# First chain rebuilt, second half's tiles normalised on GpSimd and turned behind the scores of slot 3, third unit's q products a slot later

## The chip, the cores and the metric

The kernel runs on one core of a Trainium2 chip, in one launch. The time is the device time in microseconds (us). Engines are called as the profile calls them: PE (TensorE, matrix products and turns), PEld (its weight loads), DVE (VectorE), ACT (ScalarE), POOL (GpSimd), SP (the queue that issues the transfers).

## What is computed

A transformer block with conditioned layer norms: attention over the last 512 entries of a cache, then a gated feed-forward net. S = 2048 rows of D = 512, 32 query heads on 8 key heads of 128.

```python
mod = (_silu(c) @ w_mod).reshape(c.shape[0], 6, 1, -1)
sa, ca, ga, sb, cb, gb = (mod[:, 0], mod[:, 1], mod[:, 2], mod[:, 3], mod[:, 4], mod[:, 5])
h = _layernorm(x, axis=-1) * (1 + ca) + sa
q = (h @ wq), by heads;  k, v = the last 512 rows of the caches
p = _softmax(q k^T * Dh ** -0.5);  x = x + ga * ((p v) @ wo)
h = _layernorm(x, axis=-1) * (1 + cb) + sb
x = x + gb * ((_gelu(h @ w_gate) * (h @ w_up)) @ w_down)
```

## The kernel before

Every product of two float32 matrices is made as three products of float16 halves: each operand is scaled, cut into a high half (a rounding) and a low half (what the rounding left), and `mm3` adds low by high, high by high and high by low in one PSUM bank. The scales come from norms that the kernel works out itself.

**Units and slots.** Attention is cut into units: one head times 512 rows (a quarter of the rows; the first two quarters are called first half and second half here, `qb` 0 and 1). A unit has four slots of 128 rows. The main loop runs over slots `t`: scores on PE (`ps`, two PSUM banks), the row maximum on DVE (`nm`), the exponential on ACT (`ee`), high half of `p` on ACT two slots later, low half on DVE three slots later, a transposing transfer (`pt`). Between these, `pop()` issues other products from a list: q products of coming units (`pq`), p times v (`po`), the output product (`py`). `EARLY` says how many are popped in each of the first eight slots. Everything else is put at a slot by `at(slot, fn)`: ("e", t) and ("d", t) on the way through slot t, a plain number behind its products, ("w", t) at its end. Within an engine instructions run in the order in which this code issues them.

**The first chain** is `begin()`, written out by hand; it runs from the first transfer to the first unit's q. Its steps: `silu` of the condition; the sum and factor columns `cols` of the layer norm, either by products on PE (`early_cols`, into `mps`) or by a multiply with a running sum on DVE (`mod_col`, L138); layer-norm statistics of four row tiles of the first half (`ln_stat`, `ln_power`) and the normalised tiles `xn`; their turn on PE (`turn`, into `pln`); norms of weights and k (`sumsq` on ACT, `sums` on PE); from these the scales `wsc`, `qsc`, `ksc` (`mod_scale`, `norm2`, `w_spread`); then for each of four column groups `dt` the scaled and shifted block, as float32 copy `hf` (`affine`, also written to DRAM), as high half (`direct`) and as low half (`low`); the weight's halves (`high_w`, `low_w`), k's halves, and `q_first`, in which `warm()` puts idle matmuls that keep PE going.

**The second half** needs the same for four further row tiles: `nb` holds their steps (statistics, root on GpSimd, normalisation into `xb`), `o1` the turn, copy and halves. The turn of the first column group has `fill(4)`, four idle matmuls, ahead of its third and fourth tile. The third unit (head 0, second half) is the first that needs them.

**Tables.** `PSE` names the slots whose exponential goes to a PSUM bank (tags "acc", "qa") and not to SBUF.

Of the kernel before, what the change touches and what calls it, by code (L numbers as in the profile page):

```python
# [18 lines left out]
P = 128  # L19
# [46 lines left out]
def block_kernel(ctx: ExitStack, tc: tile.TileContext, x, kT, v, wq, wo, wg, wu, wd, cT, wc, wm, out):  # L66
# [48 lines left out]
    half_ = const.tile([P, 1], F32, name="half_")  # L115
    nc.gpsimd.memset(half_, 0.5)
    ones = const.tile([P, 1], BF16, name="ones")
    nc.gpsimd.memset(ones, 1.0)
# [74 lines left out]

    def everywhere(out, m, n, fold=True):
        ps = bank("acc", "pst", NACC)
# [9 lines left out]

    def mod_scale(j, name, const_, m=None, mid=nop, between=nop):
        m, g, s = m or mod_max(j), little("mg", 2, 1), little("ms", 1, 1)
        everywhere(g, m, 2, False)
# [11 lines left out]

    def sums(m, n):
        ps = bank("acc", "pst", NACC)
        nc.tensor.matmul(ps[:, 0:n], ones.to_broadcast([P, P]), m[:, 0:n], start=True, stop=True)
        return ps
# [180 lines left out]
    def ln_first(i, act=False):  # L405
        st = {}

        def norm():
            if i < QT:
                xn[i] = tmp("xn")  # L410
                nc.vector.tensor_scalar(xn[i], acc[i], st["mv"][:, 0:1], st["rs"], op0=ALU.subtract, op1=ALU.mult)
            else:
                xn[i] = xn["b"][:, i - QT, :]
                nc.vector.tensor_scalar(xn[i], acc[i], st["mv"][:, 0:1], st["rs"], op0=ALU.subtract, op1=ALU.mult)

        def centre():
            if i < QT:
                xn[i] = tmp("xn")
            else:
                xn["b"] = pool.tile([P, QT, 512], F32, tag="pt", name="xb", bufs=NPT)  # L420
                xn[i] = xn["b"][:, 0, :]
            nc.scalar.activation(xn[i], acc[i], AF.Identity, bias=st["nm"], scale=1.0)

        def scale():
            nc.scalar.activation(xn[i], xn[i], AF.Copy, scale=st["rs"])

        pre = (lambda: ln_stat(acc[i], st, act), lambda: ln_power(st))
        return pre + ((centre, scale) if act else (norm,))

    def ln_out(qb, dt):  # L430
# [3 lines left out]

        def turn():
            st["ps"] = bank("acc", "pln", NACC)
            for i in range(QT):
                if qb and dt == 0 and i > 1:
                    fill(4)
                nc.tensor.transpose(st["ps"][:, i * P:(i + 1) * P], xn[qb * QT + i][:, dt * P:(dt + 1) * P], ident)  # L440
# [8 lines left out]

        def direct():  # L450
            nc.scalar.activation(block(0, name)[:, p, :], st["ps"], AF.Identity, scale=cols[:, 1, dt:dt + 1], bias=cols[:, 0, dt:dt + 1])

# [573 lines left out]
    def early_load(j, dt):  # L1026
        dma(wct[j][:, dt, :], wc[1, :, dt, :] if j else wm[0, dt])

# [23 lines left out]
    na = [ln_first(i, i >= 2) for i in range(QT)]  # L1052
    nb = [ln_first(QT + i, i == 0) for i in range(QT)]
    o0 = [ln_out(0, dt) for dt in range(KT)]
# [8 lines left out]
    def q_first(warm):  # L1063
        ps = bank("acc", "pq", NACC)
        for term, (a, b) in enumerate(((0, 0), (1, 0), (0, 2))):
            for kt in range(KT):
                w, m, p = SET[0][0], BK[0, ("b11", "b21")[kt // 2]], kt % 2
                nc.tensor.matmul(ps, w[:, a, kt * P:(kt + 1) * P], m[:, b + p, :], start=term + kt == 0, stop=term == 2 and kt == KT - 1)
            if term == 0:
                warm(3)  # L1070
        q_post(0, ps)

    def begin():
# [16 lines left out]
        def warm(n):  # L1090
            for _ in range(n):
                nc.tensor.matmul(wps, junk[:, 0:P], junk, start=True, stop=True)

        for dt in range(KT):
            mod_col(1, dt, wct[1][:, dt, :], sbc)
        for dt in range(KT):
            early_cols(mps, dt)
        m = {}
        pair_stat(0, m, 0)
        pair_stat(0, m, 1)  # L1100
        k0[1]()
        ts(cols[:, 1, :], cols[:, 1, :], 1.0, None, ALU.add)
        ts(cols[:, 0, :], mps[:, 0:KT], 1.0, None, ALU.mult)
        pst = {}

        def mid():
            o0[0][0]()
            pst["w"] = sums(m["m"], 2)
            o0[1][0]()
            pst["k"] = sums(k0[4]["m"], 1)  # L1110
            o0[2][0]()
            o0[3][0]()

        mod_scale(0, "ma", SCALE * TOP13 * TOP13, mod_max(0), mid)
        w = w_first(m["m"], pst["w"])
        o0[0][1](False)
        inv_k = k0[2](False, pst["k"])
        nc.vector.reciprocal(col("wsc", 0), w)
        inv_t, last = w_spread(0, m["m"], w)
        o0[0][3]()  # L1120
        high_w(0)
        for n in range(1, KT):
            o0[n][1](False)
            o0[n][3]()
            if n == 1:
                o0[0][2](nc.gpsimd)
            if n == 2:
                inv_k()
                inv_t()
                last()  # L1130
        warm(4)
        low_w(0)
        o0[1][2]()
        o0[2][2](nc.gpsimd)
        low_k = k0[3](True)
        o0[3][2]()
        low_k()
        nb[0][0]()
        nb[0][1]()
        high_w(1)  # L1140
        q_first(warm)
        v0[1]()
# [16 lines left out]
    at(("d", 4), lambda: o1[3][2]())  # L1159

# [400 lines left out]
    with tc.manual_schedule():  # L1561
        begin()
        nexty, invs = [], {}
        for t in range(T + TAIL):
# [278 lines left out]
```

## Time and profile before

| | us |
|---|---|
| median of 3 runs | 1729.52 (1729.38 to 1730.45) |
| profiled execution, device time | 1731.43 |
| its span, first to last instruction | 1729.6 |
| PE busy | 1709.0 (99% of the span) |
| DVE / ACT / POOL busy | 1426.7 / 1254.7 / 1090.0 |

Instants below are microseconds from the span's start. A profile row gives a group's start, its length, the engine, the line of the kernel, the operation, what it writes and reads, and in brackets how long the engine stood idle before it and what ended that.

### The profile page before, as it was taken

The numbers are of one execution on the slowest core, as the hardware profiler recorded it, in microseconds if no ns is written. First come the engines' busy times: TensorE is split into PE (matmuls) and PEld (weight loads), VectorE is DVE, ScalarE is ACT, GpSimd is POOL, SyncE is SP. The second block draws the span as 40 slices with busy tenths as digits, with TensorE's granted clock in tenths as the row PEclk, the third lists the DMA queues.
The fourth block names the chain that finished last, engine by engine and source line by source line (L and its number), as shares of the span: only waits on it lengthen the run. The fifth ranks groups of instructions, "written<-read, shape, count | busy, mean of one in ns | idle before, by whom it ended". The sixth has DMA issues, their size and how long they took to land.

```text
span 1729.6 us, 26339 instructions
## 1 busy us (share of the span) xinstructions
PE 1709.0 (99%) x8012; PEld 786.6 (45%) x8012; DVE 1426.7 (82%) x2476; ACT 1254.7 (73%) x2819; POOL 1090.0 (63%) x1328
## 2 busy tenths in 40 slices
PE   7999999999999999999999999999999999999999
PEld 5444444444444444444444444444444444444444
DVE  7888898888889899888788888888896788676666
ACT  6988788888888877888777877787785354455442
POOL 4879778777788984655665755757760345735424
PEclk9999999999999999999999999999999999999999
DMA  7999999999999998999999999999997556365353
GB/s 235 222 206 209 215 215 204 225 205 219 210 231 218 210 208 183 212 209 228 202 228 214 215 230 209 203 219 225 218 230 166 157 153 195 120 164 174 96 160 102
DMA packets 693454, 343.51 MB, mean 199 GB/s; under 512 B 579136, under 2 KB 602688, under 8 KB 693312
## 3 DMA queue, kind: packets, MB, share of 16 engines
q1 hardware_dynamic: 693024, 341.30, 85.7%
q8 instruction: 63, 1.03, 0.2%
q14 instruction: 79, 0.65, 0.1%
q10 hardware_dynamic: 288, 0.52, 0.1%
HBM read 137.50 MB, written 63.70 MB: 116 GB/s over the span
## 4 chain that ended last, share of the span: by engine, by line
PE 88%; DVE 4%; ACT 3%; DMA 2%; POOL 1%; issue 1%; SPq 0%; POOLq 0%; ACTq 0%; DVEq 0%
PE py L91 19%; PE po L91 17%; PE ps L91 17%; PE fa L91 8%; PE qa L91 8%; PE fc L91 4%; PE qc L91 4%; PE ya L91 3%; PE fb L91 2%; PE qb L91 2%; PE yc L91 2%; DMA pt<-p 1%; DVE p L1016 1%; ACT ee L999 1%; DVE nm L990 1%
## 5 line engine op out<-in xcount | busy, mean ns | idle before, releaser
L999 ACT ACTIVATE ee<-ps,nm 128x512 f32<-128x512 f32 x512 | 349.7, 683 | 185.6 <-DVE nm L990 180.3
L1016 DVE SCALAR_TENSOR_TENSOR p<-ee,rr,p 128x512 f16<-128x512 f32 x512 | 458.3, 895 | 8.1 <-ACT p L1011 7.6
L990 DVE TENSOR_REDUCE nm<-ps 128x1 f32<-128x512 f32 x512 | 350.3, 684 | 97.5 <-PE ps L91 95.2
L91 PE MATMUL ps<-k,qt 128*128 128x512 f16 x1536 | 414.9, 379 | 4.9 <-ACT ee L999 3.5
L1011 ACT ACTIVATE p<-ee,rr 128x512 f16<-128x512 f32 x512 | 364.0, 711 | 20.1 <-DVE rr L1007 11.3
L91 PE MATMUL po<-pt,v 128*128 128x512 f16 x1536 | 372.9, 379 | 2.6 <-DMA pt<-p 0.9
L91 PE MATMUL py<-wo,ot 128*128 128x512 f16 x1536 | 371.3, 379 | 0.0
L91 PEld LDWEIGHTS <-w 128*128 128x128 f16 x2184 | 213.5, 98 | 258.6 <-issue 0.9
L91 PEld LDWEIGHTS <-v 128*128 128x128 f16 x1536 | 150.0, 98 | 184.8 <-issue 2.8
L91 PEld LDWEIGHTS <-ot 128*128 128x128 f16 x1536 | 150.3, 98 | 181.3
L91 PEld LDWEIGHTS <-qt 128*128 128x128 f16 x1536 | 145.7, 98 | 176.4 <-issue 4.6
L1320 POOL TENSOR_TENSOR fg<-fg 128x512 f32<-128x512 f32 x48 | 62.9, 1310 | 134.6 <-DVE fg L1294 131.8
L748 DVE SCALAR_TENSOR_TENSOR ot<-po,ot 128x512 f16<-128x512 f32 x128 | 87.9, 687 | 39.2 <-ACT ot L747 38.7
L1304 ACT ACTIVATE at<-fg 128x512 f16<-128x512 f32 x92 | 56.3, 625 | 80.2 <-DVE fg L1294 60.7
L999 ACT ACTIVATION_READ_ACCUMULATOR ee<-ps,nm 128x1 f32 x512 | 100.1, 196 | 0.0
L960 DVE SCALAR_TENSOR_TENSOR acc<-py,ysc,acc 128x512 f32<-128x512 f32 x128 | 94.7, 740 | 5.3 <-PE py L91 5.3
L91 PE MATMUL qa<-t,w 128*128 128x512 f16 x348 | 84.9, 379 | 0.0
L236 POOL TENSOR_TENSOR lw<-lw,half__86 128x1 f32<-128x1 f32 x39 | 24.9, 639 | 94.7 <-DVE lw L186 94.6
L91 PE MATMUL fa<-t,w 128*128 128x512 f16 x336 | 81.6, 379 | 0.1
L747 ACT ACTIVATE ot<-po 128x512 f16<-128x512 f32 x128 | 73.9, 577 | 5.0 <-PE po L91 5.0
L403 POOL TENSOR_TENSOR rs<-rs,nhalf 128x1 f32<-128x1 f32 x32 | 18.7, 584 | 92.7 <-DVE rs L397 89.7
L91 PEld LDWEIGHTS <-wo 128*128 128x128 f16 x504 | 49.3, 98 | 59.6 <-issue 0.3
(243 smaller groups left out, 2813.8 us busy)
## 6 DMA issues: line engine op xcount, KB each, us to landing
w<-kept SPq DMA_DIRECT2D x123, 256.0 KB, 3.3
wo<-kept SPq DMA_DIRECT2D x72, 256.0 KB, 3.3
kept<-stage SPq DMA_DIRECT2D x67, 256.0 KB, 3.0
raw<-in_wo SPq DMA_DIRECT2D x56, 256.0 KB, 3.2
kept<-w SPq DMA_DIRECT2D x39, 256.0 KB, 3.4
rw<-in_wq SPq DMA_DIRECT2D x38, 256.0 KB, 3.1
hs<-hf SPq DMA_DIRECT2D x32, 256.0 KB, 2.7
pt<-p SPq DMA_TRANSPOSE x512, 3.5
```

The lines of the kernel that those rows point to most:

```text
L91: nc.tensor.matmul(ps, a, b, start=first and n == 0, stop=last and n == 2, skip_group_check=chain)
L236: nc.gpsimd.tensor_tensor(out, out, half_, op=ALU.pow)
L403: nc.gpsimd.tensor_tensor(st["rs"], st["rs"], nhalf, op=ALU.pow)
L747: nc.scalar.activation(t[:, 0, :], src, AF.Copy, scale=scale)
L748: return lambda: nc.vector.scalar_tensor_tensor(t[:, 1, :], src, scale, t[:, 0, :], op0=ALU.mult, op1=ALU.subtract)
L960: nc.vector.scalar_tensor_tensor(acc[ti], st["p"], by, acc[ti], op0=ALU.mult, op1=ALU.add)
L990: nc.vector.tensor_reduce(nm, E[t]["ps"], axis=AX.X, op=ALU.max, negate=True)
L999: nc.scalar.activation(e, E[t]["ps"], AF.Exp, bias=E[t]["nm"], scale=1.0, accum_out=sm[:, t % 2:t % 2 + 1])
L1011: nc.scalar.activation(p16[:, 0, :], E[t]["e"], AF.Copy, scale=E[t]["r"])
L1016: nc.vector.scalar_tensor_tensor(p16[:, 1, :], E[t]["e"], E[t]["r"], p16[:, 0, :], op0=ALU.mult, op1=ALU.subtract)
L1304: nc.scalar.activation(t[:, 0, :], g, AF.Copy)
L1320: nc.gpsimd.tensor_tensor(g[o], g[a], g[b], op=ALU.subtract)
```

## The change

It has four parts.

1. **Loads and columns.** Of the sum columns, two of four now come from `mod_col` on DVE and two from PE (`early_cols`), where all four came from PE; the loads are changed to match.
2. **The first chain's order.** The turns of the first half stand ahead of the scale of the columns. `mod_scale` takes two small operations fewer on DVE and works `ma` out on GpSimd. The two square roots of the weight's and k's norm are one GpSimd operation on two columns; the other small scale operations move from GpSimd to DVE. High halves come straight from PSUM first, two on ACT and two on DVE, and then the four float32 copies, all on ACT; three of four low halves are on DVE, one on GpSimd. `warm` has 6 matmuls ahead of q and its 3 stand behind the second term, not the first.
3. **The second half.** All four tiles are normalised on GpSimd (`pool_ts`); before, the first was done on ACT in two steps, its statistics within `begin()`, and three on DVE. Their steps stand in slots 0 and 1, the turn in slot 3, so behind the scores of slot 3 and not of slot 2, the copies and halves in slots 3 to 5.
4. **The third unit.** Its four q products are popped in slots 5 and 6, not 4 and 5, with their fills. Slot 5's exponential goes to SBUF.

ScalarE, in the first chain, before (`b`: halves of the first half's block, `pln`: the turned tiles, `w` and `k`: high halves of weight and k, `qt`: high half of q; `lm`: sums of squares):

```order
L219 ACTIVATE junk,lm<-raw 128x512
L451 ACTIVATE b_199<-pln,cols 128x512
L1058 ACTIVATE w_150<-rw,wsc 128x512
L451 ACTIVATE b_199<-pln,cols 128x512
L451 ACTIVATE b_200<-pln,cols 128x512 x2
L747 ACTIVATE k<-raw,ksc 128x512
L1058 ACTIVATE w_151<-rw,wsc 128x512
L747 ACTIVATE qt<-pq,qsc 128x512
```

and after:

```order
L220 ACTIVATE junk,lm<-raw 128x512
L452 ACTIVATE b_201<-pln,cols 128x512
L452 ACTIVATE b_202<-pln,cols 128x512
L1061 ACTIVATE w_152<-rw,wsc 128x512
L445 ACTIVATE hf<-pln,cols 128x512 x4
L750 ACTIVATE k<-raw,ksc 128x512
L750 ACTIVATE qt<-pq,qsc 128x512
L1061 ACTIVATE w_153<-rw,wsc 128x512
```

Two of the four direct halves have left ScalarE, the four float32 copies have come to it from VectorE, and the second weight's high half stands behind q's.

GpSimd, from the first chain's last subtraction on, before (`rs`: the roots of the second half's tiles, `y` and the later `b`: low halves of the second half, `vmax`: the scale of v):

```order
L455 TENSOR_TENSOR b_200<-hf,b_200 128x512
L403 TENSOR_TENSOR rs<-rs,nhalf 128x1 x4
L455 TENSOR_TENSOR y<-hf,y 128x512 x2
L455 TENSOR_TENSOR b_201<-hf,b_201 128x512
L236 TENSOR_TENSOR vmax<-vmax,half__86 128x1
```

and after (`xb`: the normalised tile, `mv`: its mean):

```order
L458 TENSOR_TENSOR b_201<-hf,b_201 128x512
L404 TENSOR_TENSOR rs<-rs,nhalf 128x1
L241 TENSOR_SCALAR xb<-acc,mv,rs 128x512
L404 TENSOR_TENSOR rs<-rs,nhalf 128x1
L241 TENSOR_SCALAR xb<-acc,mv,rs 128x512
L404 TENSOR_TENSOR rs<-rs,nhalf 128x1
L241 TENSOR_SCALAR xb<-acc,mv,rs 128x512
L404 TENSOR_TENSOR rs<-rs,nhalf 128x1
L241 TENSOR_SCALAR xb<-acc,mv,rs 128x512
L458 TENSOR_TENSOR y<-hf,y 128x512 x2
```

A normalisation now stands behind each root, ahead of the low halves that this queue makes.

VectorE, slots 0 to 2, before (`nm`: a slot's row maximum, `bn`, `mv`, `rs`: statistics of a tile):

```order
L990 TENSOR_REDUCE nm<-ps 128x1
L414 TENSOR_SCALAR xb<-acc,mv,rs 128x512
L393 BN_STATS bn<-acc 128x6
L395 BN_AGGR mv<-bn 128x2
L397 TENSOR_SCALAR rs<-mv 128x1
L414 TENSOR_SCALAR xb<-acc,mv,rs 128x512
L990 TENSOR_REDUCE nm<-ps 128x1
```

and after:

```order
L993 TENSOR_REDUCE nm<-ps 128x1
L394 BN_STATS bn<-acc 128x6
L396 BN_AGGR mv<-bn 128x2
L398 TENSOR_SCALAR rs<-mv 128x1
L394 BN_STATS bn<-acc 128x6
L396 BN_AGGR mv<-bn 128x2
L398 TENSOR_SCALAR rs<-mv 128x1
L993 TENSOR_REDUCE nm<-ps 128x1
```

The normalisations are gone from between the statistics.

The diff, cut to what the parts above speak of:

```diff
-PSE = dict.fromkeys((5, 7, 8, 9, 14, 18, 19, 21, 22, 23, 25, 26, 27), "acc") | dict.fromkeys((11, 15, 20, 24, 28), "qa")
-EARLY = (2, 2, 0, 0, 2, 2, 0, 0)
+PSE = dict.fromkeys((7, 8, 9, 14, 18, 19, 21, 22, 23, 25, 26, 27), "acc") | dict.fromkeys((11, 15, 20, 24, 28), "qa")
+EARLY = (2, 2, 0, 0, 0, 2, 2, 0)
...
-        nc.vector.tensor_tensor(s, g[:, 0:1], g[:, 1:2], op=ALU.add)
-        ts(s, s, FLOOR, RT / TOP13, ALU.max)
-        ts(col(name), s, const_)
-        between()
-        nc.vector.reciprocal(s, s)
-        ts(cols[:, j:j + 2, :], cols[:, j:j + 2, :], s)
+        nc.vector.tensor_scalar(s, g[:, 0:1], g[:, 1:2], FLOOR, op0=ALU.add, op1=ALU.max)
+        inv = little("mi", 1, 1)
+        nc.vector.reciprocal(inv, s)
+        ts(cols[:, j:j + 2, :], cols[:, j:j + 2, :], inv, TOP13 / RT)
+        pool_ts(col(name), s, const_ * RT / TOP13)
...
+                if i == QT:
+                    xn["b"] = pool.tile([P, QT, 512], F32, tag="pt", name="xb", bufs=NPT)
                 xn[i] = xn["b"][:, i - QT, :]
-                nc.vector.tensor_scalar(xn[i], acc[i], st["mv"][:, 0:1], st["rs"], op0=ALU.subtract, op1=ALU.mult)
+                pool_ts(xn[i], acc[i], st["mv"][:, 0:1], st["rs"], ALU.subtract, ALU.mult)
...
-        dma(wct[j][:, dt, :], wc[1, :, dt, :] if j else wm[0, dt])
+        dma(wct[j][:, dt, :], wc[j, :, dt, :] if j or dt > 1 else wm[0, dt])
...
-        for term, (a, b) in enumerate(((0, 0), (1, 0), (0, 2))):
-            for kt in range(KT):
+        for term, (a, b, kts) in enumerate(((0, 0, (0, 1, 2, 3)), (1, 0, (0, 1, 2, 3)), (0, 2, (0, 1, 2, 3)))):
+            for n, kt in enumerate(kts):
...
-            if term == 0:
+            if term == 1:
                 warm(3)
...
+        pst = bank("qa", "pst", 1)
+        for dt in (2, 3):
+            mod_col(0, dt, wct[0][:, dt, :], sbc)
+        for dt in range(2):
+            early_cols(mps, dt)
+        for tiles in ((0, 1), (2, 3)):
+            for dt in range(KT):
+                o0[dt][0](tiles)
         for dt in range(KT):
             mod_col(1, dt, wct[1][:, dt, :], sbc)
...
+        nc.gpsimd.tensor_tensor(lk, lk, half2, op=ALU.pow)
+        warm(6)
+        o0[0][3]()
+        o0[1][3](False)
+        ts(w, lk[:, 0:1], 1.005 / PRE / TOP13)
...
+        o0[2][3]()
+        o0[3][3](False)
         high_w(0)
+        low_w(0)
...
+        for n in range(KT):
+            o0[n][1]()
+        o0[0][2](nc.gpsimd)
         for n in range(1, KT):
...
+            o0[n][2]()
         low_k = k0[3](True)
...
-    at(0, nb[0][2], nb[0][3], nb[1][0], nb[1][1], nb[2][0], nb[2][1])
-    at(1, nb[1][2], nb[3][0], nb[3][1], nb[2][2])
+    at(0, *nb[0], *nb[1])
+    at(1, *nb[2], *nb[3])
...
-    at(2, nb[3][2], *[o[0] for o in o1])
+    at(3, *[o[0] for o in o1])
     for k in range(KT):
-        at(2 + k // 2, lambda k=k: o1[k][1](False), o1[k][3])
-    at(2, lambda: o1[0][2](nc.gpsimd), lambda: o1[1][2](nc.gpsimd))
-    at(3, lambda: o1[2][2](nc.gpsimd), v0[2])
-    at(("d", 4), lambda: o1[3][2]())
+        at(3 + k // 2, lambda k=k: o1[k][1](False), o1[k][3])
+    at(3, lambda: o1[0][2](nc.gpsimd), lambda: o1[1][2](nc.gpsimd))
+    at(3, v0[2])
+    at(4, lambda: o1[2][2](nc.gpsimd))
+    at(("d", 5), lambda: o1[3][2]())
...
-                if t in (4, 5):
+                if t in (5, 6):
                     fill(3)
```

More of the change, by code (lines that the diff above doesn't have):

```diff
@@ L116, in block_kernel @@
     nc.gpsimd.memset(half_, 0.5)
+    half2 = const.tile([P, 2], F32, name="half2")
+    nc.gpsimd.memset(half2, 0.5)
     ones = const.tile([P, 1], BF16, name="ones")
@@ L192, in absmax, with everywhere @@
         nc.vector.tensor_reduce(out, src, axis=AX.X, op=ALU.max, apply_absolute_value=True)
-    def everywhere(out, m, n, fold=True):
-        ps = bank("acc", "pst", NACC)
+    def everywhere(out, m, n, fold=True, ps=None):
+        ps = bank("acc", "pst", NACC) if ps is None else ps
         for i in range(n):
@@ L219, in sumsq, with sums @@
             nc.scalar.activation(junk, src, AF.Square, scale=PRE, accum_out=out)
-    def sums(m, n):
-        ps = bank("acc", "pst", NACC)
+    def sums(m, n, ps=None):
+        ps = bank("acc", "pst", NACC) if ps is None else ps
         nc.tensor.matmul(ps[:, 0:n], ones.to_broadcast([P, P]), m[:, 0:n], start=True, stop=True)
@@ L433, in ln_out, with turn @@
         st = {}
-        def turn():
-            st["ps"] = bank("acc", "pln", NACC)
-            for i in range(QT):
+        def turn(tiles=range(QT)):
+            if 0 in tiles:
+                st["ps"] = bank("acc", "pln", NACC)
+            for i in tiles:
                 if qb and dt == 0 and i > 1:
@@ L448, in affine, with direct @@
             dma(spilled(0, qb)[:, dt, :], st["f"])
-        def direct():
-            nc.scalar.activation(block(0, name)[:, p, :], st["ps"], AF.Identity, scale=cols[:, 1, dt:dt + 1], bias=cols[:, 0, dt:dt + 1])
+        def direct(act=True):
+            if act:
+                nc.scalar.activation(block(0, name)[:, p, :], st["ps"], AF.Identity, scale=cols[:, 1, dt:dt + 1], bias=cols[:, 0, dt:dt + 1])
+            else:
+                ts(block(0, name)[:, p, :], st["ps"], cols[:, 1, dt:dt + 1], cols[:, 0, dt:dt + 1], op1=ALU.add)
         def low(eng=nc.vector):
@@ L1052, in block_kernel @@
     na = [ln_first(i, i >= 2) for i in range(QT)]
-    nb = [ln_first(QT + i, i == 0) for i in range(QT)]
+    nb = [ln_first(QT + i) for i in range(QT)]
     o0 = [ln_out(0, dt) for dt in range(KT)]
@@ L1092, in warm @@
                 nc.tensor.matmul(wps, junk[:, 0:P], junk, start=True, stop=True)
+        pst = bank("qa", "pst", 1)
[6 more added lines that the diff above has]
+                o0[dt][0](tiles)
         for dt in range(KT):
             mod_col(1, dt, wct[1][:, dt, :], sbc)
-        for dt in range(KT):
-            early_cols(mps, dt)
+            if dt == 1:
+                ts(cols[:, 0, 0:2], mps[:, 0:2], 1.0, None, ALU.mult)
         m = {}
@@ L1100, in begin @@
         pair_stat(0, m, 1)
+        ts(cols[:, 1, :], cols[:, 1, :], 1.0, None, ALU.add)
+        sum_w, sum_k = pst[:, 256:258], mps[:, 2 * KT:2 * KT + 1]
+        mod_scale(0, "ma", SCALE * TOP13 * TOP13, mod_max(0), lambda: sums(m["m"], 2, sum_w), pst)
         k0[1]()
[L1102 to L1112, printed above, removed]
```

47 lines of the change are left out of this document (17 added, 30 removed).

## The prediction

> **What bounds the kernel now.** I read the page first, then the table by stretches of the opening, then the timelines of the engines there. The first two rows of the page:
>
> ```profile
> span 1729.6 us, 26339 instructions
> PE 1709.0 (99%) x8012; PEld 786.6 (45%) x8012; DVE 1426.7 (82%) x2476; ACT 1254.7 (73%) x2819; POOL 1090.0 (63%) x1328
> ```
>
> TensorE (PE) is busy for 99% of the span, so 20.6 us of idle time are all that an order of work can win; the change touches only the opening. Columns below: the stretch, its length, busy time of PE, weight loads, VectorE (DVE), ScalarE (ACT) and GpSimd (POOL).
>
> ```profile
> 20.00:25.00 5.00, 3.28 (x14) 1.18 (x13) 3.73 (x9) 2.98 (x6) 3.26 (x5) 1.00 0.80 249
> 25.00:30.00 5.00, 4.42 (x21) 1.90 (x20) 4.86 (x12) 2.91 (x8) 1.51 (x3) 1.00 0.51 176
> 30.00:35.00 5.00, 4.43 (x29) 2.65 (x28) 4.50 (x10) 3.09 (x8) 0.78 (x1) 1.00 0.00 0
> 35.00:40.00 5.00, 5.00 (x25) 2.27 (x24) 4.59 (x8) 4.63 (x11) 4.18 (x4) 1.00 0.89 244
> 40.00:45.00 5.00, 5.00 (x34) 3.31 (x33) 4.06 (x9) 4.75 (x13) 3.50 (x6) 1.00 1.13 261
> 45.00:50.00 5.00, 5.00 (x29) 2.82 (x28) 4.36 (x11) 4.74 (x13) 3.52 (x9) 1.00 1.01 213
> ```
>
> From 35 us PE does not stop for 15 us. So what counts is the instant at which PE enters that stretch with slot 4's scores; whatever it is earlier or later there, the rest carries along. In 25 to 35 us VectorE is nearly full and GpSimd nearly empty, which is where work is moved. PE's timeline of the opening (start, duration, line, output<-input, count, idle before and what ended it):
>
> ```profile
> 6.04 6.83 PE L1031 MATMUL mps<-silu,wct 128*128 128x1 f32 x32
> 13.80 1.06 PE L440 MATMUL pln<-ident,xn 128*128 128x128 f32 x4
> 17.36 1.03 PE L1092 MATMUL warm<-junk 128*128 128x512 f16 x4
> 23.26 0.59 PE L1068 MATMUL pq<-b,w 128*128 128x512 f16 x2 [0.36 <-POOL b L455]
> 24.63 0.60 PE L91 MATMUL ps<-k,qt 128*128 128x512 f16 x2 [0.78 <-DVE mv L395]
> 31.49 1.03 PE L1049 MATMUL fill<-ones 128*128 128x512 bf16 x4
> 33.09 1.64 PE L440 MATMUL pln<-ident,xb 128*128 128x128 f32 x13 [0.57 <-DVE xb L414]
> 34.56 0.81 PE L91 MATMUL ps<-k,qt 128*128 128x512 f16 x3
> 35.24 0.81 PE L91 MATMUL ps<-k,qt 128*128 128x512 f16 x3
> ```
>
> Slot 0's scores start at 24.63. The last 13 turns of the second half (`pln<-ident,xb`) wait for its last normalised tile until 33.09; then come the scores of slots 3 (34.56) and 4 (35.24).
>
> **First chain: 1.7 to 2.1 us earlier.** VectorE, ScalarE and GpSimd rows:
>
> ```profile
> 8.41 1.00 DVE L411 TENSOR_SCALAR xn<-acc,mv,rs 128x512 f32<-128x512 f32 x2
> 9.64 0.69 DVE L138 SCALAR_TENSOR_TENSOR wct<-wct,sbc 128x512 f32<-128x512 f32 x1 [0.23 <-DMA wct<-in_wc]
> 10.31 0.69 DVE L138 SCALAR_TENSOR_TENSOR wct<-wct,sbc 128x512 f32<-128x512 f32 x1
> 13.10 0.16 DVE L192 TENSOR_REDUCE mm<-cols 128x2 f32<-128x8 f32 x1
> 14.70 0.15 DVE L186 TENSOR_SCALAR ms<-ms 128x1 f32<-128x1 f32 x1
> 14.89 0.15 DVE L184 TENSOR_SCALAR ma<-ms 128x1 f32<-128x1 f32 x1
> 15.28 0.23 DVE L184 TENSOR_SCALAR cols<-cols,ms 128x8 f32<-128x8 f32 x1
> 20.40 1.28 DVE L455 TENSOR_TENSOR b<-hf,b 128x512 f16<-128x512 f32 x2
> 17.74 1.44 ACT L451 ACTIVATE b<-pln,cols 128x512 f16<-128x512 f32 x2
> 23.89 0.69 ACT L747 ACTIVATE qt<-pq,qsc 128x512 f16<-128x512 f32 x1 [0.42 <-PE pq L1068]
> 18.77 1.15 POOL L455 TENSOR_TENSOR b<-hf,b 128x512 f16<-128x512 f32 x1
> 20.50 1.23 POOL L240 TENSOR_SCALAR lr<-lr,lu 128x1 f32<-128x1 f32 x1
> 22.05 1.16 POOL L455 TENSOR_TENSOR b<-hf,b 128x512 f16<-128x512 f32 x1
> ```
>
> Up to 9.41 (8.41 + 1.00) nothing changes. Then six products L138 stand where four did, 0.68 apart (9.64, 10.31), without the 0.23 of waiting, since the first two tiles now land before: 9.41 + 4.1 + 0.35 for two small operations gives `mm` at 13.85, 0.75 later than 13.10. PE's eight fewer products of `mps` buy nothing there, for VectorE is later. Behind `pst` two small operations go, 0.19 each (14.70, 14.89), so the columns are ready at 15.51 + 0.75 − 0.38 = 15.9.
>
> From there the old path ran through GpSimd: small operations, one of them stretched to 1.23, and a subtraction (22.05 + 1.16) for which PE waited. The new path is ScalarE's row: two direct halves, the weight, four plain copies, seven operations at about 0.68 (half of 1.44, less the overlap): 15.9 + 4.8 = 20.7. Then the last subtraction, 0.64 (half of 1.28), to 21.35; the last `pq` 0.4; `qt` 0.69 and hand-overs of 0.05: slot 0's scores at 22.55. GpSimd's one remaining subtraction (1.15, near 18.8) meets VectorE's three. That VectorE and GpSimd delay each other is seen in the 1.23 at 20.50, beside VectorE's 20.40; if so here, 0.4 more. I take 22.75: **−1.9**.
>
> **The second half's tiles on GpSimd: the term that decides.** What is removed from VectorE is three operations like the first row, and from ScalarE two; what GpSimd gets is the reciprocal root (already there) and the normalisation:
>
> ```profile
> 29.27 0.54 DVE L414 TENSOR_SCALAR xb<-acc,mv,rs 128x512 f32<-128x512 f32 x1
> 24.74 0.74 DVE L748 SCALAR_TENSOR_TENSOR qt<-pq,qsc,qt 128x512 f16<-128x512 f32 x1
> 26.66 0.68 DVE L393 BATCH_NORM_STATS2 bn<-acc 128x6 f32<-128x512 f32 x1
> 27.83 0.56 POOL L403 TENSOR_TENSOR rs<-rs,nhalf 128x1 f32<-128x1 f32 x1 [2.42 <-DVE rs L397]
> L240 POOL TENSOR_SCALAR gs<-gate,osc x8: 687/692/1049, 66.8 to 580.9; 128x512 f32<-128x512 f32 x8
> L240 POOL TENSOR_SCALAR acc<-acc,mv,rs x8: 2064/2082/2520, 688.6 to 769.4; 128x512 f32<-128x512 f32 x8
> ```
>
> The last two rows are from the helper's own line (minimum/median/maximum ns). The kernel already normalises later tiles on GpSimd with the same call, subtract the mean, times the root, on 128x512 f32: 2.08 us, four times VectorE's 0.54, not the 0.69 of one product with a column. All four tiles go through one queue, so nothing overlaps.
>
> Counted from slot 0's scores: the low half of `qt`, the low half of the second weight and slot 0's maximum put the first `bn` 1.92 behind (24.74 to 26.66), and the root 1.17 behind that (27.83): 22.75 + 0.1 + 3.1 = 25.95. Each tile then costs 0.56 + 0.08 + 2.08, less a small overlap, 2.70; four make 10.8. VectorE's statistics of the other tiles, about 1 us each, stay ahead. One normalisation meets slot 0's `p` subtraction on VectorE, and the spread of the row (2.52 against 2.08) prices that at up to 0.43; I take half. The last tile is ready at 25.95 + 10.8 + 0.2 = 36.95.
>
> PE has slot 3's scores behind it by about 29 and nothing else in its order: it waits for the tiles. The fills cover 0.9 twice, no more. Then 13 turns, 1.47 (33.09 to 34.56): slot 4's scores at about 38.5, against 35.24: **+3.25** (which holds the −1.9 already). What is late next is exactly this turn; the freed VectorE and ScalarE only idle beside it.
>
> **The third unit's products a slot later: 0 to +0.4.** From slot 4's scores PE's list has the same matmuls and the same fills as before, with slot 5's scores ahead of the first product. That gives GpSimd's subtractions of the second half 0.65 more cover. At the other end `qt` of the third unit comes a slot later and stands before slot 7's exponential on ScalarE, which is 4.7 of 5 us busy there; slot 9's scores need the bank that it frees. Nothing below 0: PE had no gap here. I take **+0.35**.
>
> The rest goes with one answer: expo 5's result in SBUF instead of PSUM, the small memset, `ma` on GpSimd with no reader near, and the SP queue (the same transfers, the writes of the first half about 2 us later, their readers far off) cost nothing; ScalarE's and GpSimd's next work hides behind PE's.
>
> **The sum.** +3.25 + 0.35 = **+3.6 us**. It is made against the profiled execution, 1731.43 us (span 1729.6 and 1.8 around it); the median of the runs is 1729.52, so I forecast 1733.1, 0.21% more. A measurement of this kernel can tell about 0.2%, 3.46 us, from no change; the forecast lies just above that.
>
> The Trainium skill bears on the deciding term. "GPSIMD Engine Reference", section 4.1 (Engine selection), holds one-input elementwise work on GpSimd for roughly line-rate. This trace disagrees for this form, 2.08 against VectorE's 0.54; the rule gives the first rival.
>
> **Rivals.**
>
> *The normalisation is short (not slower), 0.10.* If these four run like `gs<-gate,osc`, 0.69, a tile takes 0.56 + 0.08 + 0.69 = 1.33: 25.95 + 5.3 = 31.25, slot 4 at 32.8, −2.4. Some of it comes back, since GpSimd's three subtractions of the second half, 1.15 each, then reach PE's products later than PE does; between 0 and 2, I put 1: −1.4, 1728.1. For it: that row, and GpSimd otherwise empty. Against it: the identical call at 2064 at the least. It decides below about 2.08 − 3.6 / 4 = 1.2 us a tile.
>
> *PE's clock rises later, 0.12.* Row 13.80 has turns 0.21 apart, row 33.09 0.11; warm-up matmuls at 17.36 run 0.216 apart, full pace. Between lie only turns, so turns raised it, and the 6.83 us of one-column products did not. Now the 16 turns stand earlier, and PE idles for over 1 us before `pst`. If the rise comes only at about 20.7, 15 matmuls of 0.216 take double, part of it under other waits: about +1.1, 1734.2. "TensorE: Matmul & The Clock Gate", Part 4 (PE-mode transpose), in the Trainium skill says that transposes do not engage the full clock; by that rule this rival would be the likely one and its time the forecast. The trace of before disagrees, as the two rows show.
>
> *PE's clock falls in the turn, 0.18.* Between 29 and 37 PE works some 2.2 of 8 us. If the clock is halved for part of what follows, from 0.5 to 3.1 us more, 1733.6 to 1736.2. Nothing in the trace shows a fall, but nothing so thin either: the thinnest stretch quoted, 20 to 25 us, has 3.28 of 5. The longest gap would be about 2.2 us.
> The Trainium skill, "TensorE: Matmul & The Clock Gate", Part 1 (The HAM clock gate), puts the fall behind gaps above about 3.4 us; by that rule it does not come, and the sum stays. No run here shows it yet.
>
> **How the numbers follow.** The forecast has 0.60, its own range 1731.6 to 1734.4 (both meetings of VectorE and GpSimd absent and no slot cost: +2.8; both full and 0.4: +4.05; and 0.7 to 0.8 for durations on each side). The range 1730.6 to 1736.3 leaves out the short normalisation and little else. Slower by over 0.2%: over half of the forecast's 0.60, and most of both clock rivals, 0.56. Within: the rest of these and nearly all of the short normalisation, 0.40. Faster by over 0.2%: 0.04.
>
> **What would show it.** Right: `xb` on GpSimd four times at about 2.1 us; PE waiting for it three times, 1.5 to 2.3 us each; slot 0's scores near 22.7 and slot 4's near 38.5. Wrong: `xb` near 0.7 or 1.2; turns or `pq` at twice their spacing behind 17 or 36; PE idle gaps after 39 that take back or add more than 0.5.

## The result, and the profile after

The changed kernel takes 1734.73 us (median of 11 runs, 1733.53 to 1736.37) and the kernel before, beside it on the same chip, 1730.35 us (11 runs, 1729.38 to 1732.57): a ratio of 1.0025 with a 95% interval of 1.0017 to 1.0034, or +4.4 us. The forecast was 1733.1, +3.6. Its base, 1729.52, was the median of three runs; over eleven runs the kernel before stands 0.8 higher, so the two differences compare better than the two times.

The head of the profile of the changed kernel, then its table by stretches (columns as in the prediction; the last three are the granted clock of PE, the DMA share and GB/s):

```profile
span 1731.7 us, 26314 instructions
PE 1710.6 (99%) x7996; PEld 784.2 (45%) x7998; DVE 1426.5 (82%) x2477; ACT 1254.6 (72%) x2819; POOL 1100.9 (64%) x1326
```

```profile
25.00:30.00 5.00, 3.85 (x18) 1.61 (x16) 4.72 (x15) 2.07 (x7) 4.16 (x4) 1.00 0.77 284
30.00:35.00 5.00, 2.83 (x7) 1.05 (x9) 1.75 (x4) 2.65 (x7) 4.79 (x5) 0.65 0.29 56
35.00:40.00 5.00, 4.47 (x22) 2.93 (x21) 1.96 (x4) 1.90 (x3) 2.73 (x2) 0.66 0.20 74
```

The work has moved as planned: in 30 to 35 us VectorE falls from 4.50 to 1.75 and GpSimd rises from 0.78 to 4.79. PE falls with VectorE, from 4.43 to 2.83: it waits for the engine that was made busy. GpSimd's timeline names the work, PE's the waits:

```profile
25.61 0.55 POOL L404 TENSOR_TENSOR rs<-rs,nhalf 128x1 f32<-128x1 f32 x1 [6.10 <-DVE rs L398]
26.27 2.08 POOL L241 TENSOR_SCALAR xb<-acc,mv,rs 128x512 f32<-128x512 f32 x1
31.71 2.19 POOL L241 TENSOR_SCALAR xb<-acc,mv,rs 128x512 f32<-128x512 f32 x1
34.53 2.08 POOL L241 TENSOR_SCALAR xb<-acc,mv,rs 128x512 f32<-128x512 f32 x1
```

```profile
22.47 0.60 PE L91 MATMUL ps<-k,qt 128*128 128x512 f16 x2 [0.78 <-ACT qt L750]
31.13 0.33 PE L440 MATMUL pln<-ident,xb 128*128 128x128 f32 x1 [2.28 <-POOL xb L241]
33.96 0.48 PE L440 MATMUL pln<-ident,xb 128*128 128x128 f32 x1 [0.98 <-POOL xb L241]
36.67 2.44 PE L440 MATMUL pln<-ident,xb 128*128 128x128 f32 x13 [0.53 <-POOL xb L241]
38.97 1.45 PE L91 MATMUL ps<-k,qt 128*128 128x512 f16 x6
52.26 0.81 PE L91 MATMUL ps<-k,qt 128*128 128x512 f16 x3
```

Slot 0's scores start 2.16 earlier (22.47 for 24.63), slot 4's 3.73 later (38.97 for 35.24) and slot 9's 4.11 later (52.26; before they stood at 48.15, first row below). The 13 last turns took 2.44 where they took 1.64. The table by stretches, cut at the clock's own steps, shows why:

```profile
48.15 0.81 PE L91 MATMUL ps<-k,qt 128*128 128x512 f16 x3
```

```profile
28.12:31.53 3.41, 1.07 (x6) 0.51 (x6) 3.14 (x8) 2.34 (x5) 3.29 (x4) 1.00 0.22 85
31.53:34.95 3.42, 2.44 (x6) 0.78 (x6) 0.42 (x1) 1.11 (x4) 3.21 (x4) 0.50 0.42 81
34.95:38.36 3.41, 2.88 (x11) 1.85 (x10) 1.14 (x2) 0.33 (x1) 1.66 (x1) 0.50 0.00 0
```

PE's clock was halved from 31.53 to 38.36, behind a stretch in which PE worked 1.07 of 3.41 us. A loss of clock is no accident of the profiled execution: the granted clock, averaged over a whole run, is 0.998 or less in all 11 runs of the changed kernel, and 0.999 or 1.0 in 86 of the 96 runs of the kernel before beside the experiments. Where in a run it was lost, these averages do not say.

The two profiled executions end 2.1 us apart (1733.53 and 1731.43), less than the medians; that of before lies 1.1 above its median and that of after 1.2 below. The better guide is the lag at slot 9: how much later slot 9's scores start than in the kernel before, ahead of what later stretches of either execution add. The table below puts it beside the medians of all kernels tried; each difference is against the runs of before on the same chip. Slots are the starts of their first scores in us. Slots and lag come from one profiled execution of each kernel, the medians from 11 runs (second_only: 5).

| kernel | slot 0 | slot 4 | slot 9 | lag at 9 | median, difference | ratio, 95% interval |
|---|---|---|---|---|---|---|
| before | 24.63 | 35.24 | 48.15 | 0 | | |
| after | 22.47 | 38.97 | 52.26 | +4.11 | +4.4 | 1.0025 [1.0017, 1.0034] |
| chain_only | 22.52 | 33.46 | 46.37 | -1.78 | -1.3 | 0.9993 [0.9984, 1.0002] |
| second_only | 24.65 | 41.23 | 54.52 | +6.37 | +6.6 | 1.0037 [1.0024, 1.0049] |
| norm_on_vector | 22.75 | 36.24 | 49.60 | +1.45 | +1.1 | 1.0007 [0.9998, 1.0015] |
| more_fill | 22.44 | 38.03 | 52.34 | +4.19 | +3.7 | 1.0022 [1.0013, 1.0031] |
| mult_add | 22.58 | 34.65 | 48.98 | +0.83 | +0.1 | 1.0 [0.9992, 1.0009] |
| sub_only | 22.44 | 37.25 | 51.55 | +3.40 | +3.3 | 1.002 [1.0011, 1.0028] |
| norm_split | 23.21 | 35.10 | 50.28 | +2.13 | +1.3 | 1.0007 [0.9998, 1.0016] |
| chain_third | 22.32 | 34.36 | 49.02 | +0.87 | -0.2 | 1.0 [0.9991, 1.0009] |
| mult_add_vec | 22.83 | 34.97 | 48.26 | +0.11 | -0.8 | 0.9996 [0.9987, 1.0005] |
| chain_mixed | 22.25 | 33.74 | 46.65 | -1.50 | -0.6 | 0.9996 [0.9987, 1.0005] |
| chain_mixed2 | 22.61 | 34.45 | 47.35 | -0.80 | -1.3 | 0.9989 [0.998, 0.9998] |

The lag at slot 9 and the difference of the medians agree to within 1.1 us in every row, so the opening decides, as the prediction had it.

### The profile page after: what moved, and what is told of

It is laid out like the page before. It is cut to its first block, busy times and chain, and to the rows that moved or that the text cites. A ratio compares the mean times of both kernels' runs of the same rounds, so it can differ in the third digit from the quotient of the medians.

```text
span 1731.7 us, 26314 instructions
## 1 busy us (share of the span) xinstructions
PE 1710.6 (99%) x7996; PEld 784.2 (45%) x7998; DVE 1426.5 (82%) x2477; ACT 1254.6 (72%) x2819; POOL 1100.9 (64%) x1326
## 4 chain that ended last, share of the span: by engine, by line
PE 88%; DVE 4%; ACT 4%; POOL 1%; issue 1%; DMA 1%; ACTq 0%; POOLq 0%; DVEq 0%
PE py L91 19%; PE po L91 17%; PE ps L91 17%; PE fa L91 8%; PE qa L91 8%; PE fc L91 4%; PE qc L91 4%; PE ya L91 3%; PE qb L91 2%; PE fb L91 2%; PE yc L91 2%; ACT ee L1002 1%; DVE p L1019 1%; DVE nm L993 1%; PE pq L91 1%
```

## The experiments

**The change taken apart.** Three kernels undo parts of it.

chain_only keeps the rebuilt first chain and puts all else back:

```diff
-EARLY = (2, 2, 0, 0, 0, 2, 2, 0)
+EARLY = (2, 2, 0, 0, 2, 2, 0, 0)
...
-                pool_ts(xn[i], acc[i], st["mv"][:, 0:1], st["rs"], ALU.subtract, ALU.mult)
+                nc.vector.tensor_scalar(xn[i], acc[i], st["mv"][:, 0:1], st["rs"], op0=ALU.subtract, op1=ALU.mult)
...
-    at(0, *nb[0], *nb[1])
-    at(1, *nb[2], *nb[3])
+    at(0, nb[0][2], nb[0][3], nb[1][0], nb[1][1], nb[2][0], nb[2][1])
+    at(1, nb[1][2], nb[3][0], nb[3][1], nb[2][2])
```

> After, with the second half's steps, the turn's slot and the third unit's products put back to where before has them; only the rebuilt first chain is left. Theory: slot 0's scores near 22.5, the turn's last tile some 1.2 to 2 us earlier than before, and the whole 1.2 to 2.2 us faster than before. Rival (the chain's gain is lost in the turn, which waits for VectorE anyway): same time as before within 0.5 us.

second_only is the opposite: the kernel before with the second half's and the third unit's lines of the change.

> Before's first chain with the other parts of the change: normalisation on GpSimd, turn behind slot 3, third unit a slot later, slot 5's exponential in SBUF. Theory: everything of after from slot 0 on, but 2.2 us later, so slot 4's scores near 41 and 5 to 6.5 us slower than before. Rival (the chain's gain and the turn's loss do not add up): about as slow as after, +4.

norm_on_vector is the changed kernel with the engine of the normalisation alone put back (and the order in which VectorE then takes the tiles):

```diff
-                pool_ts(xn[i], acc[i], st["mv"][:, 0:1], st["rs"], ALU.subtract, ALU.mult)
+                nc.vector.tensor_scalar(xn[i], acc[i], st["mv"][:, 0:1], st["rs"], op0=ALU.subtract, op1=ALU.mult)
...
-    at(0, *nb[0], *nb[1])
-    at(1, *nb[2], *nb[3])
+    at(0, *nb[0][:2], *nb[1][:2])
+    at(1, nb[0][2], *nb[2][:2], nb[1][2], *nb[3][:2])
+    at(2, nb[2][2], nb[3][2])
```

> After, with one thing undone: the second half's four tiles are normalised on VectorE again, one or two slots behind their statistics; the chain, the turn behind slot 3 and the third unit's place stay. Theory (GpSimd's 2.1 us a tile sets the turn): the last tile is ready near 32 and not at 36.6, slot 4's scores start near 34.5, slot 9's near 48, so -0.5 to +0.5 us against before and 4 us less than after. Rival (the late turn and the late products are what costs): it stays 2 us or more above before.

Measured: -1.3, +6.6 and +1.1; the intervals of the first and the last include no difference. By slot 9 the first chain gains and the second half loses, and the engine of the normalisation alone is worth 2.7 us at slot 4 and at slot 9 (38.97 and 52.26 against 36.24 and 49.60). From chain_only to after 5.89 us are lost at slot 9; norm_on_vector, 3.23 behind chain_only, keeps the other 3.2, which belong to the order of the steps, the turn's place with the clock's fall in it, and the third unit, not taken apart further. The +1.1 that norm_on_vector keeps was not expected: with the tiles on VectorE and the turn behind slot 3's scores, PE still waits for a tile, and its clock still halves. PE's timeline there:

```profile
32.10 0.48 PE L440 MATMUL pln<-ident,xb 128*128 128x128 f32 x1 [1.58 <-DVE xb L417]
34.08 2.30 PE L440 MATMUL pln<-ident,xb 128*128 128x128 f32 x13
```

**What makes 2.08 us.** mult_add writes the same normalisation as a product and a sum:

```diff
+            st["mr"] = small.tile([P, 1], F32, name="mr") if i >= QT else None
...
-                pool_ts(xn[i], acc[i], st["mv"][:, 0:1], st["rs"], ALU.subtract, ALU.mult)
+                pool_ts(st["mr"], st["mv"][:, 0:1], st["rs"], -1.0)
+                pool_ts(xn[i], acc[i], st["rs"], st["mr"], ALU.mult, ALU.add)
```

> The changed kernel with the second half's tiles on GpSimd as x*rs + (-mean*rs), a product and a sum with two columns, in place of (x - mean)*rs; one small product of about 0.2 us goes ahead of each tile. Theory A, that GpSimd's 2.08 us come from the second column: still 2.08 a tile, 2.9 to 3.0 us from tile to tile, slot 4's scores 1.0 us later than in the changed kernel, +5 against the kernel before. Theory B, that they come from the subtraction: near 0.7 to 1.1 a tile, and slot 4's scores 3 to 4 us earlier, near +0.5 or below.

sub_only takes the subtraction by itself:

```diff
-                pool_ts(xn[i], acc[i], st["mv"][:, 0:1], st["rs"], ALU.subtract, ALU.mult)
+                pool_ts(xn[i], acc[i], st["mv"][:, 0:1], 1.0, ALU.subtract, ALU.mult)
```

> The changed kernel with the second half's tiles on GpSimd as (x - mean)*1, one column and a constant; the product with the root is left out. Theory A (the second column costs): 0.69 a tile as in the row of gs, 1.33 from tile to tile, the last tile ready near 31.0, slot 4's scores near 32.8 and the third unit's products waiting for GpSimd: -1.4 against the kernel before, as the rival of the short normalisation has it. Theory B (the subtraction costs): 2.08 a tile, slot 4's scores at 38.9 and the time of the changed kernel, +3.8 to +4.4.

The tile's rows in after, mult_add and sub_only (minimum/median/maximum ns, first and last start):

```profile
L241 POOL TENSOR_SCALAR xb<-acc,mv,rs x4: 2075/2081/2194, 26.3 to 34.5; 128x512 f32<-128x512 f32 x4
```

```profile
L241 POOL TENSOR_SCALAR xb<-acc,rs,mr x4: 762/762/762, 26.7 to 32.3; 128x512 f32<-128x512 f32 x4
```

```profile
L241 POOL TENSOR_SCALAR xb<-acc,mv x4: 1999/2001/2010, 26.1 to 33.7; 128x512 f32<-128x512 f32 x4
```

Theory B holds: one subtraction of a column takes 2.00, two columns as product and sum 0.76. It is the subtraction that costs, not the second column. Whether an addition put first would be short was not tried; the short form has the product first. (sub_only's slot 4, 37.25, is below the 38.9 of its expectation: 2.52 from tile to tile, and 13 turns at full clock, 1.64.) In mult_add the time went to +0.1, slot 4's scores to 34.65, 0.59 before the kernel before. Yet slot 9's came 0.83 after it. PE's and GpSimd's timelines of mult_add show what took it back:

```profile
41.31 0.38 PE L91 MATMUL pq<-b,w 128*128 128x512 f16 x1 [0.88 <-POOL b L460]
```

```profile
35.24 2.72 POOL L460 TENSOR_TENSOR y<-hf,y 128x512 f16<-128x512 f32 x2 [2.16 <-ACT y L454]
39.11 2.15 POOL L460 TENSOR_TENSOR b<-hf,b 128x512 f16<-128x512 f32 x1
```

PE is early enough now to meet the low parts of the second half (`low`), which GpSimd computes in one queue.

mult_add_vec moves the third of them to VectorE:

```diff
-    at(4, lambda: o1[2][2](nc.gpsimd))
+    at(4, lambda: o1[2][2]())
```

> The changed kernel with the tiles as product and sum on GpSimd (0.76 us each there), and the third block's low part of the second half on VectorE in place of GpSimd. With the short tiles slot 4's scores came at 34.65, 0.59 before the kernel before, and slot 9's 0.82 behind it: PE had waited 0.88 for that low part (b on GpSimd, 2.15 us, begun at 39.11 and finished at 41.26). If GpSimd's low part is what takes the gain back, that wait goes, VectorE's own b (0.68) is ready in time, slot 9's scores come within 0.2 of the kernel before, and the time is -0.7 below the kernel with the short tiles. If VectorE, 4.5 of 5 us busy there, is late with the extra 0.65 instead, slot 9 stays at +0.6 to +0.9 and the time with it.

The wait went, and from slot 4 to slot 9 it is 13.29 us again as in after; the lag at slot 9 is 0.11, the median 1730.08 for 1730.90 (-0.8, with no difference inside the interval).

**Half the tiles on each engine.** norm_split:

```diff
-                pool_ts(xn[i], acc[i], st["mv"][:, 0:1], st["rs"], ALU.subtract, ALU.mult)
+                if i % 2 == 0:
+                    pool_ts(xn[i], acc[i], st["mv"][:, 0:1], st["rs"], ALU.subtract, ALU.mult)
+                else:
+                    nc.vector.tensor_scalar(xn[i], acc[i], st["mv"][:, 0:1], st["rs"], op0=ALU.subtract, op1=ALU.mult)
...
-    at(0, *nb[0], *nb[1])
-    at(1, *nb[2], *nb[3])
+    at(0, *nb[0], *nb[1][:2])
+    at(1, *nb[2][:2], nb[1][2], nb[2][2], *nb[3][:2])
+    at(2, nb[3][2])
```

> The changed kernel with two of the second half's four tiles normalised on GpSimd (the first and the third) and two on VectorE, in this order of the program. If GpSimd's one queue of four tiles sets slot 4's scores, they come as the two queues allow: the third tile ready near 31.2, the fourth near 32.5 on VectorE behind slot 2's maximum; slot 4's scores near 34.5 to 36, +0.2 to +1.2 against the kernel before, some 3 us below the changed kernel. If the place of the turn behind slot 3's scores set it, they would stay near 39 and the time at +4. PE's clock: with PE idle half of a 3.41 us stretch behind 28, halved for one such stretch; no idle gap above 2.3 us.

Slot 4 came at 35.10 and not near 39, so the queue of four set it, not the turn's place. PE then waited 1.19 for GpSimd's low part, as in mult_add, and slot 9 was 2.13 late. The halved stretch that was expected in the turn did not come. But in this execution the clock came up late: its first full-clock record starts at 20.58 (17.88 in after), and the stretches of the table that lie ahead of a trace's first record read 1.00 without one. PE's rows show the half pace there:

```profile
14.88 2.72 PE L1098 MATMUL warm<-junk 128*128 128x512 f16 x6
17.54 3.38 PE L1074 MATMUL pq<-b,w 128*128 128x512 f16 x8
```

The eight `pq` took 3.38 where they take 2.04 in after. VectorE's last low half for them came at the same time in both (21.2 to 21.3), yet slot 0's scores started at 23.21 for 22.47. So norm_split lost 0.74 at slot 0 to the clock's late rise and not to its tiles; how much of this is left in its lag at slot 9 is open.

**The clock in the turn.** more_fill fills PE's waits:

```diff
-                if qb and dt == 0 and i > 1:
-                    fill(4)
+                if qb and dt == 0 and i > 0:
+                    fill(9)
```

> After, with nine idle matmuls ahead of the second, third and fourth tile of the first group's turn, where it has four ahead of the third and fourth. Theory (the clock's fall costs 0.8 us on the 13 turns and nothing else): the granted clock stays at full through 28 to 40, the turns run 0.11 apart, slot 4's scores start 0.8 earlier, so 0.8 us less than after, near +3.4 against before. Rival (the fall costs nothing, or the fills themselves delay the tiles' turns): same as after or slower.

The clock stayed full in the turn and the 13 turns took 1.64 again; slot 4 came 0.94 earlier than in after. But slot 9 did not (52.34 for 52.26). The medians, +3.7 where +3.4 was expected and after has +4.4, cannot tell: their intervals overlap. PE's timeline, then the table by stretches of the same kernel:

```profile
36.53 1.64 PE L440 MATMUL pln<-ident,xb 128*128 128x128 f32 x13
44.68 0.38 PE L91 MATMUL pq<-b,w 128*128 128x512 f16 x1 [0.86 <-POOL b L458]
```

```profile
20.51:23.92 3.41, 1.91 (x7) 0.35 (x6) 2.89 (x6) 2.16 (x5) 0.00 (x0) 1.00 0.95 263
23.92:27.33 3.41, 3.41 (x9) 1.21 (x10) 2.38 (x7) 0.78 (x2) 1.64 (x2) 0.50 0.93 296
```

The same wait for a low part took the 0.94 back: that part began 0.89 earlier than in after (42.49 for 43.38), but behind VectorE's `p`, and took 2.14 for 1.15. And the clock halved elsewhere, at 23.92, where its program is still that of after.

**The third unit a slot later, by itself.** chain_third is chain_only with the three lines of it:

```diff
-EARLY = (2, 2, 0, 0, 2, 2, 0, 0)
+EARLY = (2, 2, 0, 0, 0, 2, 2, 0)
...
-                if t in (4, 5):
+                if t in (5, 6):
```

(and slot 5's result in SBUF, as in the change.)

> The rebuilt first chain alone with the third unit's products a slot later (their place in the order of slots, the fills that go with them and slot 5's result in SBUF), the second half's tiles as in the kernel before. If the slot costs what the sum gave it: slot 9's scores 13.3 us behind slot 4's, where the chain alone has 12.91, and the time 0.35 above the chain alone's -1.3, near -0.95. Rival: the extra 0.4 belongs to the turn behind slot 3, then 12.9 and -1.3.

Neither figure held: 14.66 us from slot 4 to slot 9, and -0.2. PE's timeline, slot 5's scores:

```profile
36.09 0.81 PE L91 MATMUL ps<-k,qt 128*128 128x512 f16 x3 [0.92 <-ACT ee L1006]
```

Slot 5's scores now stand right behind slot 4's and wait 0.92 for ScalarE's exponential of an earlier slot, whose bank they need. That and a shorter such wait of slot 6's scores make 1.37 of the 1.75; the other 0.37 are lost at slot 8, which waits for the third unit's `qt`, as in the changed kernel. In the changed kernel ScalarE's last exponential before the turn ended at 31.74, over 7 us before slot 5's scores. ScalarE's row there:

```profile
31.07 0.67 ACT L1002 ACTIVATE ee<-ps,nm 128x512 f32<-128x512 f32 x1
```

**A faster version.** chain_mixed is chain_only with the third tile on GpSimd as product and sum:

```diff
+                if i == QT + 2:
+                    st["mr"] = small.tile([P, 1], F32, name="mr")
+                    pool_ts(st["mr"], st["mv"][:, 0:1], st["rs"], -1.0)
+                    pool_ts(xn[i], acc[i], st["rs"], st["mr"], ALU.mult, ALU.add)
+                else:
+                    nc.vector.tensor_scalar(xn[i], acc[i], st["mv"][:, 0:1], st["rs"], op0=ALU.subtract, op1=ALU.mult)
```

> The rebuilt first chain alone, the second half as in the kernel before, with one of its four tiles (the third) on GpSimd as product and sum. The chain alone had PE waiting 0.57 for VectorE's last tile, the two tiles before it at 28.94 and 30.73 on VectorE. If GpSimd's 0.76 and 0.27 fit behind its third root (27.7 to 28.7) and before its fourth (29.2), the last tile is ready 0.4 to 0.5 earlier, PE's wait is 0.1, slot 4's scores come near 33.0 and the time is 0.4 below the chain alone, -1.7 against the kernel before. If GpSimd and VectorE hold each other up, the fourth root is late and nothing is won: -1.3.

-0.6: the tile stood behind the fourth root in GpSimd's queue, and PE waited for it. chain_mixed2 turns the two round:

```diff
-    at(1, nb[1][2], nb[3][0], nb[3][1], nb[2][2])
+    at(1, nb[2][2], nb[1][2], nb[3][0], nb[3][1])
```

> The kernel before this one, with the third tile's product and sum on GpSimd put ahead of the fourth tile's root there. In the kernel before this one the tile stood behind that root (28.89) and came at 30.55, so that PE waited 1.32 for it and nothing was won. Now the tile can start with its own root's end (27.4), is ready near 28.5, and the fourth root still starts near 28.9: the last tile, on VectorE, sets the turn, ready near 30.6 to 30.9 where the chain alone had 31.26; slot 4's scores near 33.0, 0.4 before the chain alone, which would be the fastest of all: -1.7 against the kernel before. If the two engines hold each other up instead, -1.3 or above.

PE's rows of chain_mixed, then GpSimd's and PE's of chain_mixed2:

```profile
30.61 0.33 PE L449 MATMUL pln<-ident,xb 128*128 128x128 f32 x1 [1.32 <-POOL xb L241]
```

```profile
28.23 0.77 POOL L241 TENSOR_SCALAR xb<-acc,rs,mr 128x512 f32<-128x512 f32 x1
30.55 0.55 POOL L404 TENSOR_TENSOR rs<-rs,nhalf 128x1 f32<-128x1 f32 x1 [1.56 <-DVE rs L398]
24.51 2.74 PE L91 MATMUL pq<-b,w 128*128 128x512 f16 x6 [0.27 <-DVE w L1073]
```

The tile came in time, but the time is -1.3 where -1.7 was forecast, the figure that the expectation gave to two engines holding each other up. What held the fourth root to 30.55 (28.9 was expected) was VectorE's statistics, late behind slot 1's scores: in this profiled execution the six `pq` at 24.51 ran at the halved clock (2.74 for the 1.47 they take in after), so its slot 4 is no measure of the order; over 11 runs it has the lowest ratio of all, 1729.14 us against 1730.46, 0.9989 [0.998, 0.9998]. It beats after, and before by an interval that just leaves out no change; that it beats chain_only (0.9993 [0.9984, 1.0002]) the intervals do not show.

## Why the prediction was right, and where it was not

*The bound.* Right: what PE enters slot 4 with, the rest carries.

*First chain, -1.9.* Right. VectorE's and PE's rows of the changed kernel there:

```profile
9.79 0.69 DVE L140 SCALAR_TENSOR_TENSOR wct<-wct,sbc 128x512 f32<-128x512 f32 x1
10.40 0.69 DVE L140 SCALAR_TENSOR_TENSOR wct<-wct,sbc 128x512 f32<-128x512 f32 x1
13.23 0.16 DVE L194 TENSOR_REDUCE mm<-cols 128x2 f32<-128x8 f32 x1
17.56 2.04 PE L1071 MATMUL pq<-b,w 128*128 128x512 f16 x8
```

PE has sixteen products of `mps` fewer, not the eight of the prediction, which changes nothing, since VectorE is later. VectorE's six products stand 0.61 apart, not 0.68, and begin 0.2 earlier, so `mm` came at 13.23 where 13.85 was forecast; some of that was lost again behind it, and slot 0 had its scores at 22.47, forecast 22.75. The chain by itself is worth -1.78 at slot 9 and -1.3 in the median, whose interval does not exclude none; inside the change it is 4.4 less 6.6.

*The second half, +3.25.* The tiles came as worked out: 2.08, 2.08, 2.19, 2.08, with 2.7 to 2.8 from one to the next, and the predicted meeting with VectorE's `p` is the 2.19. The last was ready at 36.61 (36.95 forecast). The turns behind it were mis-sized: slot 4 followed the start of the 13 turns by 2.30, not 1.47, since the clock had halved. So the sum's +3.25 was +3.73, the slower turn less the sooner tile. The three waits for tiles were 2.28, 0.98 and 0.53, where 1.5 to 2.3 each was the sign of being right: at half clock the fills between them took 1.46 and 1.91, not 0.9.

*The clock rivals.* The fall in the turn, with 0.18, came true beside the forecast, and with it one of the signs of being wrong, turns at twice their spacing behind 36. It cost 0.8 there. That more_fill took this back without moving slot 9 shows that it was not on the path to the end: without it PE would have waited for GpSimd's low part instead. The prediction set the fall's price of 0.5 to 3.1 on top of the sum, and overlooked that cover. The Trainium skill, "TensorE: Matmul & The Clock Gate", Part 1 (The HAM clock gate), lets the clock fall behind gaps above about 3.4 us. The trace does not agree: the longest wait was 2.28 us, and in more_fill no wait of the stretch ahead of the fall was above 0.78. The other rival, the late rise with 0.12, did not cost here: the clock came up at 17.88 (before: 17.28), and the six `warm` at 14.88 ran at half pace (2.72), but the eight `pq` behind them needed the weight's high half, which ScalarE finished at 17.51, and took 2.04 (row above), full pace. In norm_split's execution it did come true, at 20.58 where the prediction had "about 20.7", and cost 0.74 at slot 0, for the 1.1 that it had put.

*The short normalisation, 0.10.* It did not come, but the reason given, "the identical call at 2064 at the least", named the call and not what in it costs. With the subtraction avoided (mult_add) the tile is short, and the rival's sum can be held against a run. What comes back was sized right: from slot 4 to slot 9 1.42 was lost (-0.59 to +0.83), of it 0.38 as in after and 1.04 by GpSimd's low part, for which 1 was put. The gain itself was mis-sized, -2.4 forecast at slot 4 and -0.59 measured. This form needs a small product ahead of each tile, which the rival's call did not, so the tiles came 1.86 apart and not 1.33; one root also waited 0.30 for VectorE's statistics:

```profile
26.37 0.26 POOL L241 TENSOR_SCALAR mr<-mv,rs 128x1 f32<-128x1 f32 x1
```

The Trainium skill, "GPSIMD Engine Reference", section 4.1, has one-input work at roughly line-rate; 0.76 beside VectorE's 0.54 is near that for product and sum, 2.00 for a subtraction is not.

*The third unit, +0.35.* Measured +0.38 (13.29 for 12.91 between slots 4 and 9), but not by the mechanism that was put. The prediction had slot 9's scores wait for a bank that ScalarE frees late. They do not wait; PE stops at the third unit's own first scores, slot 8's, for the low half of its `qt`, which VectorE makes:

```profile
49.28 0.39 PE L91 MATMUL ps<-k,qt 128*128 128x512 f16 x1 [0.21 <-DVE qt L751]
```

That third product starts 0.80 behind the first where 0.43 is the pace: 0.37 lost. That the size fits is luck. Without the late turn the same move cost 1.75 (14.66), since slots 5 and 6 then wait for their banks too. The prediction's "PE had no gap here" holds where PE's wait in the turn has covered slot 5's wait for its bank.

*The total.* +4.11 at slot 9 and +4.4 in the median, where 3.6 was forecast. By the sum's terms the difference at slot 9 is the clock in the turn (0.8) less the earlier tile (0.3). Taking the fall away would not have closed it: with the clock up in the turn, in more_fill, slot 9 had the same lag (+4.19) by the wait for GpSimd's low part, which the sum had at nothing, since it gave these parts 0.65 more cover.

## What to carry to other kernels

Before work is moved to an idle engine, look for the row of the very same operation there, and ask which part of it makes the price: here a subtraction rewritten as product and sum took 0.76 us for 2.08, and with it the changed kernel's loss of 4.4 us fell to 0.1. Prices found one by one do not add: the third unit's move cost 0.38 behind a late turn and 1.75 behind an early one, and a gain of 0.94 in the turn was gone five slots later, because one wait had covered the next. And a size that fits does not show that its mechanism does: the +0.35 came true at another wait than the one it was made from.

## What the runs showed of the hardware that was not expected

In these traces PE's clock went by how much of a stretch PE had worked, not by a single long gap. Once it had risen, every halved stretch in these traces, but for the end of the program, lasted 3.41 us or 6.83, twice that. Reckoning on from the clock's steps in pieces of 3.41 us, it fell behind all five pieces in which PE was busy 0.44 or less (0.32 in after), behind some between 0.45 and 0.57, and behind none at 0.58 or above. The last 8 us of the program are left out: there two pieces at 0.42, in before and mult_add, had no fall behind them. Matmul ends are modelled, so these shares are rough, and no run was made to test the rule. Where the pieces begin changes from execution to execution: chain_only halved at 15.63 and chain_third at 23.66, with the same program up to there, and the first rise came anywhere from 12.00 (chain_mixed) to 20.58 (norm_split) with the same rebuilt chain. A thin place in PE's work is so a draw: the same six `pq` behind slot 0's scores took 1.47 in after and 2.74 in chain_mixed2.

VectorE and GpSimd hold each other up, and which of them is held is a matter of who starts first. In after GpSimd's low part began before VectorE's `p`, took 1.15, and `p` was stretched; in mult_add `p` was ahead, kept its 0.74, and GpSimd's low part took 2.15. So it went in the other executions where the two meet here: with `p` ahead GpSimd's part took 2.14 to 2.15 in more_fill, norm_split and sub_only. The two rows of after, from the timelines of GpSimd and VectorE, then VectorE's of mult_add (GpSimd's stands above):

```profile
43.38 1.15 POOL L458 TENSOR_TENSOR b<-hf,b 128x512 f16<-128x512 f32 x1 [0.69 <-ACT b L452]
43.67 1.42 DVE L1019 SCALAR_TENSOR_TENSOR p<-ee,rr,p 128x512 f16<-128x512 f32 x1
```

```profile
38.91 0.74 DVE L1021 SCALAR_TENSOR_TENSOR p<-ee,rr,p 128x512 f16<-128x512 f32 x1
39.57 0.68 DVE L460 TENSOR_TENSOR b<-hf,b 128x512 f16<-128x512 f32 x1
```
